# A diffusion block: the first modulation in two column parts, and one block turned by DMA

## The chip, the cores and the metric

The kernel runs on one core of a Trainium2 chip. The metric is device time in microseconds, the median of several executions. The engines are PE (TensorE matmuls), PEld (its weight loads), DVE (VectorE), ACT (ScalarE), POOL (GpSimd) and SP (SyncE, which here only issues transfers; ACT issues some too).

## The reference

One token block of a diffusion transformer with adaptive layer norm: 2048 tokens, width 640, 32 heads of 20, a sliding window of 256 keys, and a gated MLP of width 1536. Cut to what matters:

```python
mod = (silu(c) @ w_mod).reshape(1, 6, 1, 640)     # c: 1 x 640, w_mod: 640 x 3840
sa, ca, ga, sb, cb, gb = the six parts of mod
h = layernorm(x) * (1 + ca) + sa                   # first modulation: sa and ca
qkv = h @ wqkv                                     # 640 x 1920, q, k, v of 32 heads
p = softmax(mask(q k' / sqrt(20)))                 # causal, 256 keys back
x = x + ga * ((p v) @ wo)
h = layernorm(x) * (1 + cb) + sb                   # second modulation
x = x + gb * ((sigmoid(h @ w_gate) * (h @ w_up)) @ w_down)
```

## The kernel before, in words

The 2048 tokens are worked on in eight chunks of 256, each of two blocks of 128 (block 0 and block 1). For a chunk: layer norm of both blocks with tokens on partitions, a turn to `hT` (features on partitions, five tiles `dt` of 128), the modulation as a scale and a shift per partition, the projections to q, k and v (token blocks times weight halves of 320 columns), a turn of q and k to `QT` and `KT`, scores, exponential, masks, the product with V, normalization, output projection, second norm, and the MLP. Chunks overlap: the projections of the next two chunks and the MLP of earlier ones are interleaved on PE with the scores.

The order of the work is not found at run time and not by the loops. The loops only record operations with their reads and writes, each on an engine or a choice of engines. `PLAN` (L365) is a table of numbers that gives for every step which recorded operation comes next and on which engine; `schedule` walks the table and `emit` turns it into one program per engine, with semaphore waits worked out from the reads and writes. So each engine works strictly in its own order, and what waits blocks what stands behind it. SP's transfers stand in one queue in order of issue. The table has one entry for each of some 2000 operations.

What the change touches, by lines of the kernel before:

- `load_x` (L606) loads a block of x; the first two go out at once, one from SP and one from ACT. `load_bulk` (L621) loads weights in pieces by input tile. The first modulation's 1280 columns of `w_mod` (shift and scale, 640 each) come in five pieces of 128 x 1280 (L646) into the room of `wd`, which is free then.
- `load_w3` (L632) loads wq: tiles 0 to 2 of the left half first of all, then the right half, then tiles 3 and 4 of the left half.
- `silubc` (L662 to L669) is silu(c), turned by PE (`ctr`), halved by DVE into `c_col`, through a tanh on ACT and a product on DVE, and spread to 64 columns on ACT.
- `warm` (L676) is matmuls on zeros at the start, `fill` (L687) single ones on zeros between the first real steps.
- `modA` (L760 to L779): for each of five input tiles `kt`, ten 64-column matmuls of `w_mod` against `silubc` into one PSUM tile; then one DVE copy to `mA`, five shift columns and five scale columns.
- `pe_transposes` (L843) turns chunk 0 and 1's normalized x on PE through `ident`; `modulate` (L825) applies `mA` to chunk 0 in 128 x 128 pieces on DVE, ACT or POOL.
- `qkv` (L929) does the projections through `pe_chain` (L701), whose `step` says how many of the five input tiles stand in one PE operation, and turns q and k: on PE with an evacuation by ACT or DVE for chunks below `NPQ`, with a DMA transpose issued by SP for all others.
- Every plain matmul is recorded at L698, every one that uses a part of the array at L699, every plain DMA at L584, every DMA transpose at L822.

## Time and profile before

| what | value |
|---|---|
| median of 3 runs | 323.93 us (322.73 to 323.95) |
| profiled execution, first to last instruction | 321.83 us |
| median less that span | 2.1 us |
| PE busy | 315.6 us, 98% of the span, 5045 matmuls |
| DVE, ACT, POOL busy | 198.8, 213.9, 189.5 us |
| DMA | 32.92 MB, mean 102 GB/s |

The profiled execution's own time is its span, 321.83 us; the runs' times are device times that lie around such a span. PE is busy nearly throughout, so its busy share alone says little: what is to be looked for is where it is not busy, and which work is on it that could be elsewhere. The page's slices of 8 us show the DMA share at nine tenths or more up to about 88 us and then at a few tenths.

### The profile page before, as it was taken

What the parts mean: (1) busy time and instruction counts of PE and PEld (TensorE: products, weight loads), DVE (VectorE), ACT (ScalarE), POOL (GpSimd) and SP (SyncE); (2) the same over time, 40 slices, a digit from 0 to 9 for tenths busy, and PEclk for the clock granted to TensorE, in tenths of its full rate; (3) what the DMA queues carried; (4) which work ended last, traced back from release to release, by engine and by line L of the source; (5) the groups of instructions that cost most, each with busy time, mean ns of one, the idle gap of its engine ahead of it and who ended that gap; (6) DMA issues with size and microseconds to landing.
All of it is one profiled execution on the core that took longest, in us unless ns stands there. A gap on an engine that the chain in (4) does not pass through costs nothing.

```text
span 321.8 us, 11465 instructions
## 1 busy us (share of the span) xinstructions
PE 315.6 (98%) x5045; PEld 236.8 (74%) x5045; DVE 198.8 (62%) x424; ACT 213.9 (66%) x229; POOL 189.5 (59%) x349
## 2 busy tenths in 40 slices
PE   6999999999999999999999999999999999999996
PEld 2677767677877777766777677877877777877885
DVE  4689987877886746584555555465534474386323
ACT  2699997877787986768686867676976746411220
POOL 3338759878768493949484848577575826601000
PEclk9999999999999999999999999999999999999999
DMA  7999999999922534126526100220800004002101
GB/s 249 348 262 278 223 179 248 194 225 295 206 36 43 88 75 55 44 63 108 77 19 111 37 22 2 63 42 25 132 18 4 22 22 104 20 5 61 43 0 41
DMA packets 62123, 32.92 MB, mean 102 GB/s; under 512 B 45946, under 2 KB 60794, under 8 KB 62074
## 3 DMA queue, kind: packets, MB, share of 16 engines
q1 hardware_dynamic: 59904, 29.73, 43.5%
q10 hardware_dynamic: 2170, 2.46, 2.8%
q8 instruction: 39, 0.64, 0.9%
q14 instruction: 10, 0.08, 0.1%
HBM read 18.68 MB, written 2.62 MB: 66 GB/s over the span
## 4 chain that ended last, share of the span: by engine, by line
PE 96%; DMA 1%; DVE 1%; ACT 1%; issue 0%; ACTq 0%
PE M L698 79%; PE S L699 8%; PE M L699 7%; DMA x<-in_A_x_dram 1%; ACT hT L831 1%; DVE st L793 1%; PE S L698 1%; PE S L690 0%; ACT stg L914 0%; ACTq L584 0%; DVE x L815 0%; DVE st L795 0%; ACT hT L914 0%; DVE x L1308 0%; DVE mA L778 0%
## 5 line engine op out<-in xcount | busy, mean ns | idle before, releaser
L1067 ACT ACTIVATE E<-S 128x2048 bf16<-128x2048 f32 x56 | 105.0, 1875 | 40.6 <-PE S L699 40.2
L1072 POOL TENSOR_SCALAR_AFFINE_SELECT E<-E 128x256 bf16<-128x256 bf16 x112 | 46.6, 427 | 57.1 <-ACT E L1067 25.1
L1076 POOL TENSOR_SCALAR_AFFINE_SELECT E<-E 128x512 bf16<-128x512 bf16 x112 | 70.6, 646 | 4.6 <-DVE x L815 1.2
L698 PE MATMUL M<-h2T,wg 128*128 128x256 bf16 x480 | 67.0, 273 | 0.0
L698 PE MATMUL M<-h2T,wu 128*128 128x256 bf16 x480 | 66.7, 273 | 0.0
L1289 DVE SCALAR_TENSOR_TENSOR hh<-sig,M 128x512 bf16<-128x512 f32 x48 | 32.4, 678 | 42.9 <-ACT sig L1287 26.4
L698 PE MATMUL M<-wd,hh 128*128 128x320 bf16 (+2 forms) x396 | 57.1, 295 | 0.0
L698 PEld LDWEIGHTS M<-h2T,wg 128*128 128x128 bf16 x480 | 45.4, 98 | 7.8 <-DVE T L1162 0.2
L698 PEld LDWEIGHTS M<-h2T,wu 128*128 128x128 bf16 x480 | 45.2, 98 | 7.3
L1287 ACT ACTIVATE sig<-M 128x512 f32<-128x512 f32 x48 | 28.5, 595 | 31.2 <-PE M L698 30.9
L698 PEld LDWEIGHTS M<-wd,hh 128*128 128x128 bf16 x396 | 37.2, 98 | 13.7 <-DVE hh L1289 0.2
L1045 POOL TENSOR_SCALAR_AFFINE_SELECT E<-E 128x1024 bf16<-128x1024 bf16 x28 | 32.0, 1147 | 4.9 <-ACT E L1041 3.4
L699 PEld LDWEIGHTS S<-QT,KT 20*64 20x64 bf16 (+1 forms) x1856 | 20.0, 100 | 17.4 <-issue 9.7
L699 PE MATMUL S<-QT,KT 20*64 20x256 bf16 (+5 forms) x1856 | 32.3, 228 | 0.4 <-issue 0.4
L1041 ACT ACTIVATE E<-S 128x2048 bf16<-128x2048 f32 x14 | 26.3, 1876 | 6.8 <-PE S L699 6.7
L793 DVE BATCH_NORM_STATS2 st<-x 128x6 f32<-128x320 bf16 x64 | 28.9, 479 | 2.4 <-DMA x<-in_A_x_dram 1.8
L1162 DVE STREAM_TRANSPOSE T<-M 128x512 f32<-128x512 f32 x32 | 21.5, 700 | 12.9 <-PE S L699 11.6
L698 PE MATMUL M<-wk,hT 128*128 128x320 bf16 x160 | 27.9, 299 | 0.0
L1308 DVE TENSOR_TENSOR x<-M,x 128x320 bf16<-128x320 f32 (+2 forms) x33 | 15.4, 475 | 18.8 <-PE M L698 18.6
L698 PE MATMUL M<-wq,hT 128*128 128x320 bf16 x160 | 26.2, 299 | 0.7 <-DVE hT L832 0.5
L698 PE MATMUL M<-wv,hT 128*128 128x320 bf16 x160 | 26.0, 299 | 0.0
L698 PE MATMUL M<-wo,oT 128*128 128x320 bf16 x160 | 25.9, 299 | 0.0
(84 smaller groups left out, 356.4 us busy)
## 6 DMA issues: line engine op xcount, KB each, us to landing
x<-in_A_x_dram SPq DMA_DIRECT2D x18, 160.0 KB, 3.7
wd<-in_w_mod_dram SPq DMA_DIRECT2D x6, 320.0 KB, 5.4
wd<-in_B_w_down_dram SPq DMA_DIRECT2D x4, 480.0 KB, 5.5
wu<-in_w_mod_dram SPq DMA_DIRECT2D x5, 320.0 KB, 4.8
x<-in_A_x_dram ACTq DMA_DIRECT2D x8, 160.0 KB, 2.7
out_dram<-x SPq DMA_DIRECT2D x8, 160.0 KB, 1.9
wu<-in_B_w_up_dram SPq DMA_DIRECT2D x2, 576.0 KB, 4.7
wg<-in_B_w_gate_dram SPq DMA_DIRECT2D x2, 576.0 KB, 6.8
```

The source lines that it names most:

```text
L698: return e.matmul(o, l, r, start=st, stop=sp, skip_group_check=True)
L699: return e.matmul(o, l, r, start=st, stop=sp, tile_position=tp, skip_group_check=True)
L793: A("dve", lambda e, g, bi=bi, j=j: e.bn_stats(v(bi * 12 + j * 6, 6), src[bi].ap[:, j * 320:(j + 1) * 320]), 0.48, reads=[src[bi].r()], wr ...
L1041: A("act", lambda e, eng: e.activation(cell().rearrange("p m (x c) -> p m x c", c=64)[:, :, 0:4:3, :], Sp.ap[:].rearrange("p j (k x c) -> ...
L1045: A("pool", lambda e, eng, c0=c0, pat=pat, base=base, cm=cm: e.affine_select(cell()[:, :, c0:c0 + 64], cell()[:, :, c0:c0 + 64], pattern=p ...
L1067: A("act", lambda e, eng: e.activation(part(0, 512), Sp.ap[:], ACT.Exp, scale=SM_SCALE), 1.876, reads=[Sp.r()], writes=[E.r("C"), E.r("B") ...
L1072: A("pool", lambda e, eng, hc=hc, src=src, far_h=far_h: e.affine_select(side(hc), part(src, 64), pattern=[[0, 4], [-1 if far_h else 1, 64] ...
L1076: A("pool", lambda e, eng, c0=c0, near=near: e.affine_select(part(c0, 128), part(c0, 128), pattern=[[0, 4], [1 if near else -1, 128]], com ...
L1162: A("dve", lambda e, g, h=h: e.transpose(T1.ap[:, 512 * h:512 * h + 512], X[h].ap), 0.694, reads=[X[h].r()], writes=[T1.r(h)], prio=3.5, t ...
L1287: A("act", lambda e, g, pg=pg, sg=sg: e.activation(sg.ap[:], pg.ap[:], ACT.Tanh, scale=0.5), c_act(512), reads=[pg.r()], writes=[sg.r()], ...
L1289: A("dve", lambda e, g, pu=pu, sg=sg, f0=f0: e.scalar_tensor_tensor(out=hh.ap[:, f0:f0 + 2, :], in0=sg.ap[:].rearrange("p (a b) -> p a b", ...
L1308: A("dve", lambda e, g, ps=ps, bi=bi, c0=c0, n=n: e.tensor_tensor(x1[bi].ap[:, c0:c0 + n], ps.ap[:, 0:n], x1[bi].ap[:, c0:c0 + n], op=ALU. ...
```

## The change

- The first modulation is split by columns into tiles 0 to 2 (part 0, `CUT = 3`) and tiles 3 and 4 (part 1): in loading (six transfers in place of five, rows of 768 and 512 bytes in place of 2560), in multiplying (thirty matmuls, then twenty, each part with its own PSUM accumulation and its own copy to `mA`) and in applying (an operation on tile `dt` reads the copy of its part only).
- wq is loaded as tiles 0 to 2 in full width ahead of everything, and tiles 3 and 4 in full width later. Chunk 0's Q projection on PE is made in steps of three and two tiles.
- The warm-ups are seven groups with sixteen matmuls in place of eleven. The column `c_col` is gone: the tanh and the product read PSUM, with the half as a scale.
- PE turns q and k of chunk 0 and of chunk 1's block 1 (in the code's count, from 0); the other block of chunk 1, its first, is now turned by DMA.
- `PLAN` is another table for all engines. The planner's costs and latencies (`dlat`, durations of modulations and warm-ups) were changed too; they have no effect at run time besides the table.

Places where the order moves. First PE, from the turns of chunk 0's x to the first K projection; `S<-E` is warm-up and fill, `S<-silubc,wd` is `modA`, `M<-ident,x` turns x, `M<-ident,stg` turns q and k. Before:

```order
L690 MATMUL S<-E 128x512
L698 MATMUL M<-ident,x 128x128 x2
L690 MATMUL S<-E 128x512 x2
L698 MATMUL M<-ident,x 128x128 x3
L698 MATMUL S<-silubc,wd 128x64 x30
L690 MATMUL S<-E 128x512 x2
L698 MATMUL M<-wq,hT 128x320 x17
L698 MATMUL M<-ident,stg 128x128 x8
L698 MATMUL M<-wq,hT 128x320 x3
L698 MATMUL M<-wk,hT 128x320 x5
```

Now:

```order
L713 MATMUL M<-ident,x 128x128 x5
L713 MATMUL S<-silubc,wd 128x64 x12
L705 MATMUL S<-E 128x512 x2
L713 MATMUL M<-ident,x 128x128 x5
L705 MATMUL S<-E 128x512 x2
L713 MATMUL M<-wq,hT 128x320 x6
L713 MATMUL S<-silubc,wd 128x64 x20
L705 MATMUL S<-E 128x512
L713 MATMUL M<-wq,hT 128x320 x14
L713 MATMUL M<-wk,hT 128x320 x5
L713 MATMUL M<-ident,stg 128x128 x12
```

Six Q matmuls now stand ahead of part 1's twenty, all twenty Q matmuls stand ahead of any turn of q, and the eight turns that stood ahead of the first K projection now stand behind it.

Second, SP's queue at the start. Before:

```order
L584 DMA wq<-in_A_wqkv_dram 128x3x320
L584 DMA x<-in_A_x_dram 128x640
L584 DMA wd<-in_w_mod_dram 128x1280 x5
L584 DMA wq<-in_A_wqkv_dram 128x5x320
L584 DMA wq<-in_A_wqkv_dram 128x2x320
L584 DMA x<-in_A_x_dram 128x640 x2
L584 DMA wk<-in_A_wqkv_dram 128x5x320
```

Now:

```order
L590 DMA wq<-in_A_wqkv_dram 128x3x640
L590 DMA x<-in_A_x_dram 128x640
L590 DMA wd<-in_w_mod_dram 128x3x384 x2
L590 DMA wd<-in_w_mod_dram 128x2x384 x2
L590 DMA x<-in_A_x_dram 128x640
L590 DMA wd<-in_w_mod_dram 128x5x256 x2
L590 DMA x<-in_A_x_dram 128x640
L590 DMA wq<-in_A_wqkv_dram 128x2x640
L590 DMA wk<-in_A_wqkv_dram 128x5x320 x2
```

The first wq load is twice as large and ahead of x, part 0 follows x, and a block of x stands ahead of part 1 and another ahead of the rest of wq.

Third, SP further on, where the first DMA transposes stand. Before:

```order
L584 DMA wo<-in_A_wo_dram 16x3x640
L584 DMA wd<-in_w_mod_dram 128x3x640
L822 DMA_TRANSPOSE hT<-x 128x5x128 x2
L584 DMA wd<-in_w_mod_dram 128x2x640
L584 DMA gate<-grow 4x160
```

Now:

```order
L590 DMA wu<-in_w_mod_dram 128x1280 x2
L843 DMA_TRANSPOSE QT<-stg 128x8x128
L590 DMA wd<-in_w_mod_dram 128x3x640
L843 DMA_TRANSPOSE KT<-stg 128x8x128
L590 DMA hh<-in_w_mod_dram 128x3x640
L843 DMA_TRANSPOSE hT<-x 128x5x128 x2
L590 DMA wd<-in_w_mod_dram 128x2x640
L590 DMA gate<-grow 4x160
```

Two turns, of q and of k of chunk 1's first block, with loads between them, now stand ahead of the turn of chunk 2's `hT`.

The diff, cut to its core; of the table only one line:

```diff
 PLAN = [
-    119, 53, 76, 3, 8, 297, 86, 84, 300, 305, 333, 270, 277, 99, 281, 48, 442, 335, 28, 437, 447, 94, 13, 287, 422, 427,
...
-NPQ = 2
-PQ = ()
+NPQ = 1
+CUT = 3
+PQ = ((1, "q", 1), (1, "k", 1))
...
         if k == "wq":
-            for t0, t1 in ((0, 3), (3, 5)):
-                dma(lambda t0=t0, t1=t1: W3[k][:, t0:t1, 0:320], lambda t0=t0, t1=t1: wqkv_src[:, t0:t1, 0:320], 0.224 * (t1 - t0),
+            for t0, t1 in ((0, CUT), (CUT, NDT)):
+                dma(lambda t0=t0, t1=t1: W3[k][:, t0:t1, :], lambda t0=t0, t1=t1: wqkv_src[:, t0:t1, 0:D], 0.448 * (t1 - t0),
                     writes=R_wq0[t0:t1], prio=prio, tag=k)
...
-    load_bulk(wm_ap[0], wm_src[:, :, 0:1280], Rm[0], 0.88, 0.2, "wm0", dlat=2.89)
+    Rw = [[[R(f"wm0_{part}_{kt}_{b}") for kt in range(NDT)] for b in range(2)] for part in range(2)]
+    for part, (lo, hi) in enumerate(((0, 128 * CUT), (128 * CUT, D))):
+        k = 0
+        for m in (3, 5) if part == 0 else (5,):
+            for b in (1, 0):
+                dma(lambda k=k, m=m, lo=lo, hi=hi, b=b: wm_ap[0][:, k:m, b * D + lo:b * D + hi],
+                    lambda k=k, m=m, lo=lo, hi=hi, b=b: wm_src[:, k:m, b * D + lo:b * D + hi],
...
-    A("dve", lambda e, g: e.tensor_scalar(c_col[:], psc.ap[:, 0:NDT], 0.5, None, op0=ALU.mult), 0.17, reads=[psc.r()], writes=[R_ccol], prio=0)
-    A("act", lambda e, g: e.activation(cth[:], c_col[:], ACT.Tanh), 0.2, reads=[R_ccol], writes=[R_cth], prio=0)
+    A("act", lambda e, g: e.activation(cth[:], psc.ap[:, 0:NDT], ACT.Tanh, scale=0.5), 0.21, reads=[psc.r()], writes=[R_cth], prio=0)
...
-    for i in range(6):
-        o = A("pe", warm if i < 5 else lambda e, g: warm(e, g, 1), 1.03 if i < 5 else 0.52, prio=90, reads=[R_z], extra=wprev, tag="warm", writes=[R("w")])
+    for d, n in ((0.92, 2), (0.92, 2), (0.92, 2), (0.7, 2), (0.5, 2), (0.45, 2), (0.86, 4)):
+        o = A("pe", lambda e, g, n=n: warm(e, g, n), d, prio=90, reads=[R_z], extra=wprev, tag="warm", writes=[R("w")])
...
+    SPAN = ((0, CUT), (CUT, NDT))
...
+    for part, (lo, hi) in enumerate(SPAN):
+        n = (hi - lo) * MW
+        for kt in range(NDT):
+            def fnA(e, g, kt=kt, lo=lo, hi=hi, part=part, n=n):
+                for b in (1, 0):
+                    for cg in range(lo, hi):
+                        ins = mm(e, psA.ap[:, part, b * n + (cg - lo) * MW:b * n + (cg - lo + 1) * MW],
+                                 wm_ap[0][:, kt, b * D + cg * 128:b * D + cg * 128 + 128], silubc[:, kt, 0:MW], False, kt == NDT - 1)
+                return ins
+            if kt and part == 0:
+                fills.append(fill(FILL, oA[-1:]))
...
+        A("dve", lambda e, g, lo=lo, hi=hi, part=part, n=n: e.tensor_copy(
+            mA[:, :, lo:hi], psA.ap[:, part, 0:2 * n].rearrange("p (b a m) -> p b a m", b=2, m=MW)[:, :, :, 0]), 0.17,
+          reads=[psA.r(part)], writes=[R_mA[part]], prio=0)
...
-                A(MOE, mb, {"dve": 0.24, "act": 0.42, "pool": 0.38}, port=True, reads=Rmod, writes=[dst.r((dt, bi))], prio=prio,
+                A(MOE, mb, {"dve": 0.31, "act": 0.48, "pool": 0.45}, port=True, reads=[Rmod[dt >= CUT]] if len(Rmod) > 1 else Rmod, writes=[dst.r((dt, bi))], prio=prio,
...
-                             hold=[s, dst] + (pss if PAIR else []))
+                             hold=[s, dst] + (pss if PAIR else []), step=CUT if a == 0 and key == "q" else 2)
```

## The prediction

> **What bounds the kernel now.** I read the busy times of all engines by stage first, since the page's averages mix stages with different limits. Columns: the stretch in us, its length, busy us of PE, PEld, DVE, ACT, POOL with their instruction counts, granted clock, DMA share, GB/s.

> ```profile
> 1.31:6.00 4.69, 4.67 (x13) 1.46 (x13) 1.32 (x6) 1.49 (x2) 1.15 (x7) 1.00 0.84 263
> 6.00:7.47 1.47, 0.00 (x0) 0.00 (x0) 1.44 (x5) 0.47 (x1) 0.82 (x2) 1.00 1.03 368
> 7.47:11.22 3.75, 3.75 (x66) 2.56 (x66) 1.44 (x6) 1.07 (x3) 1.35 (x5) 1.00 1.08 375
> 11.22:11.71 0.49, 0.00 (x0) 0.03 (x1) 0.49 (x3) 0.49 (x2) 0.00 (x0) 1.00 1.14 367
> 11.71:13.95 2.24, 2.08 (x15) 1.31 (x16) 1.56 (x5) 2.09 (x6) 1.32 (x3) 1.00 1.15 320
> 15.19:60.00 44.81, 44.41 (x788) 31.33 (x786) 38.37 (x91) 40.06 (x49) 31.20 (x56) 1.00 1.09 237
> 60.00:319.40 259.40, 259.40 (x4153) 199.05 (x4151) 152.69 (x309) 167.59 (x167) 152.68 (x268) 1.00 0.34 68
> 319.40:321.83 2.43, 0.01 (x1) 0.00 (x0) 0.29 (x1) 0.00 (x0) 0.00 (x0) 1.00 0.26 81
> ```

> From 15.19 us, where the first K projection starts, to 319.4 TensorE is busy in all but 0.40 us, at the full granted clock. No other engine can be the bound there. So a time can come only from three places: when that dense stretch begins, how much PE work is in it, and new holes. The tail of 2.43 us ends with the same last add and store in both programs. In the dense stretch's first 45 us the DMA share is also at 1.09, so transfers are a second limit just behind PE.

> Second view, the waits, PE alone, from 13.9 us on: these two are all there are.

> ```profile
> PE S L699 <- issue: 0.4, 1, 0.4
> PE M L698 <- ACT stg L914: 0.2, 1, 0.2
> ```

> Third, what sets the beginning: issue times from the timeline, and time from issue to landing from the transfers of short windows.

> ```profile
> 1.82 2.34 SPq L584 DMA_DIRECT2D wd<-in_w_mod_dram  x5
> wd<-in_w_mod_dram SPq DMA_DIRECT2D x1, 320.0 KB, 5.1
> wd<-in_w_mod_dram SPq DMA_DIRECT2D x1, 320.0 KB, 6.5
> 7.54 0.45 SPq L584 DMA_DIRECT2D wk<-in_A_wqkv_dram  x1
> wk<-in_A_wqkv_dram SPq DMA_DIRECT2D x1, 400.0 KB, 6.7
> 10.83 0.17 DVE L778 COPY mA<-S 128x10 f32<-128x10 f32 x1 [1.46 <-PE S L698]
> 15.19 0.84 PE L698 MATMUL M<-wk,hT 128*128 128x320 bf16 x5
> ```

> The first of five modulation loads (the row of 5.1) is issued at 1.82 and lands at 6.9. The last (6.5) is issued near 3.7, because five issues share 2.34 us, and lands at 10.2. The modulation is copied out at 10.83, 0.6 later. The first K weights land at 7.54 + 6.7 = 14.2. Now bytes. Ahead of the first modulation landing lie 240 KB of wq, 320 KB of x and itself, 0.90 MB; ahead of the last 2.21 MB; ahead of the K weights 3.52 MB. So 1.31 MB of 2560-byte rows took 3.3 us (400 GB/s), and the next 1.31 MB, of 640- and 1280-byte rows, 4.0 us (327 GB/s). These two rates bound the changed loads, whose rows have 1280, 768 and 512 bytes.

> **The change part by part.** Loads first. The new order on SP is wq 480 KB, x, the modulation's columns 0 to 383 (576 KB, then 384 KB), block 2 of x, columns 384 to 639 (640 KB), block 3, the rest of wq (320 KB), K weights. Counting on from 0.90 MB landed at 6.9: part 0 is complete at 1.80 MB, which is 9.2 at 400 GB/s and 9.7 at 327; part 1 at 2.62 MB, 11.2 or 12.2; the rest of wq at 3.11 MB, 12.4 or 13.7; the K weights at 3.52 MB, 13.5 or 14.9. I take the slower rate, whose 640-byte rows are nearest in size, and shade it by 0.1. Part 0 is thus half a microsecond earlier than the whole was, and part 1 two later. [...]

> Then PE, from these rows (their starts give spacings):

> ```profile
> 7.80 0.47 PE L698 MATMUL S<-silubc,wd 128*128 128x64 bf16 x10
> 8.10 0.38 PE L690 MATMUL S<-E 128*128 128x512 bf16 x1
> 8.32 0.45 PE L698 MATMUL S<-silubc,wd 128*128 128x64 bf16 x10
> 14.34 0.61 PE L698 MATMUL M<-ident,stg 128*128 128x128 bf16 x8
> 14.79 0.57 PE L698 MATMUL M<-wq,hT 128*128 128x320 bf16 x3
> 15.87 0.33 PE L698 MATMUL M<-ident,stg 128*128 128x128 bf16 x3
> L831 ACT ACTIVATE hT<-hT,mA x4: 479/487/493, 11.0 to 12.7; 128x128 bf16<-128x128 bf16 x4
> L832 POOL TENSOR_SCALAR hT<-hT,mA x3: 452/452/453, 12.5 to 13.3; 128x128 bf16<-128x128 bf16 x3
> ```

> Ten modulation matmuls take 0.30, a fill 0.22, eight transposes 0.45 (0.056 each), five 320-column matmuls 15.19 to 15.87, 0.137 each. In the new order part 1's twenty matmuls (0.6) follow the first six Q matmuls. From part 1's landing at 12.1: twenty, 0.6; fill, 0.22; six Q matmuls of the second block, 0.82; eight of columns 3 and 4, 1.1. That gives 14.85, and with two semaphore steps, up to 15.1 for the first K matmul. The K weights, landing at 14.8, allow 14.9. Beside this lie the copy of part 1 (0.17) and the four remaining modulations, two each on ACT (0.49) and POOL (0.45), some 1.1 in all, against 1.04 of fill and Q matmuls: they fit, and cost about 0.1 if they do not. The c column that is no longer written, the product moved to DVE and the five more warm-ups end before part 0 lands; x lands 0.6 to 0.75 later behind the doubled wq, and its second block is normalized near 10, before the PE reaches its transposes. So they cost nothing, covered by the wait for part 0; without that cover the late x would cost its 0.7. **First term:** 15.19 becomes 15.1, -0.1 (14.6 to 15.9).

> **Second term.** Sixteen Q and K transposes of the first block of chunk 1 leave PE. But before, eight transposes of chunk 0 stood ahead of the first K matmul, and now none does. Inside the dense stretch 56 become 48: eight fewer, -0.45. The freed evacuations, about 0.6 each, lie on DVE and ACT beside PE and bring nothing by themselves. Changes between PE's four-row form and the full one are 154 in both orders, so the rest of the dense work is equal.

> **Third term,** new holes. The score tile has one buffer, and the next scores wait for the exponential of the last.

> ```profile
> 29.37 1.88 ACT L1104 ACTIVATE E<-S 128x2048 bf16<-128x2048 f32 x1 [0.43 <-PE S L699]
> 28.98 0.33 PE S L699 x8
> 31.33 0.37 PE S L699 x16
> 33.88 0.36 PE S L699 x24
> ```

> Scores start 2.35 and 2.55 apart here. Priced from the rows, the new order places two sets of chunk 0 and the first of chunk 1 about 2.25 apart; two times 0.1 is missing. I take +0.2 (0 to 1.5, the upper end if each of the first fifteen sets loses 0.1).

> Sum: -0.1 - 0.45 + 0.2 = -0.35. The profiled execution has a span of 321.83; the median run, 323.93, stands 2.1 above it, which I keep outside as unchanged. **Forecast 323.6 us.** A measurement of this kernel can tell about 0.5% (1.6 us) from no change, so this counts as the same.

> **Rivals.** First, the other side: the DMA turn is late. The scores of chunk 1 read K of its first block, and behind the waiting score matmul all of PE is queued.

> ```profile
> 29.32 1.47 PE M L699 x72
> hT<-x SPq DMA_TRANSPOSE x1, 6.5
> KT<-stg SPq DMA_TRANSPOSE x1, 4.3
> 33.81 0.43 PE L699 MATMUL S<-QT,KT 20*64 20x256 bf16 x24
> ```

> From the first K matmul to this first score of chunk 1 took 18.6; the new order has two projection matmuls more and eight transposes fewer, 18.45, so it is due at 33.55. Behind the last K matmul of that block stand 29 projection matmuls (4.0), eight transposes (0.45), three score sets (1.1) and the 72 matmuls of 1.47: it ends at 26.5, its evacuation about 0.7 later, and the turn, behind one more load on SP, is issued at 27.4. With 4.3 to 6.5 to landing it comes at 31.7 to 33.9: just hidden. Each us beyond 33.55 is paid in full. Slower than before from a landing at 34.0 on; at 8.5 us, two more than the longest here, 35.9 and **325.9**. For it: the DMA share of 1.09. Against: the rows.

> Second: transfers keep 400 GB/s. Part 1 at 11.2 lets PE pace the stage and K start at 14.6; if the 0.40 of instruction waiting also falls elsewhere, -0.6 - 0.45 - 0.4 + 0.1 gives **322.6**. [...]

> Third, the clock. Spacing of the warm-up matmuls' weight loads:

> ```profile
> 3.91 0.15 PEld L679 LDWEIGHTS S<-E 128*128 128x128 bf16 x1 [0.28 <-issue]
> 4.34 0.15 PEld L679 LDWEIGHTS S<-E 128*128 128x128 bf16 x1 [0.28 <-issue]
> ```

> They start 0.43 apart, half the speed of the 0.22 fill. If executions open at different times, eleven warm-ups may at times be too few, and the runs' spread (322.73 to 323.95) would be that; a longer warm-up, 1.31 to about 6.8 by eight matmuls of 0.43 and eight of 0.22, would give the fast run each time, 322.73 - 0.35 = **322.4**. For it: two of three runs lie together high. Against: this execution was at full speed before its work began. [...]

> Fourth: 512-byte rows go slower than any here, say 260 GB/s for part 1 (0.66 MB, 2.5 instead of 2.0) with the loads behind: K starts at 15.9, **324.4**.

> **How the numbers follow.** Forecast 0.50, late turn 0.14, quick transfers 0.13, clock 0.13, slow rows 0.10. Below 322.3 fall about a third to half of the two fast cases, 0.13 with the forecast's edge; above 325.5 three quarters of the late turn and the edges, 0.14; the rest, 0.73, is the same. The forecast's own range is 322.9 to 324.5. Reaching to the others until about 0.2 is left out gives 322.1 to 325.3.

> **What would show it.** Right: first K matmul at 14.9 to 15.3, 48 transposes left, no PE wait over 0.3 after it. Part 1's matmuls at 12 to 12.3 confirm the transfer rate; at 11.3 the second rival. A PE wait ahead of the first chunk 1 score shows the late turn. Wrong: a hole over 1 us in the dense stretch anywhere, or a K start outside 14.6 to 15.9.

## The result, and the profile after

| | before | changed |
|---|---|---|
| median of 6 runs, us | 323.22 (322.53 to 323.95) | 331.63 (329.06 to 333.49) |
| span of the profiled execution, us | 321.8 | 329.3 (its own time 331.06) |
| first K matmul, us | 15.19 | 14.50 |
| `ident,stg` transposes | 64 | 48 |

The ratio is 1.0243 (95% interval 1.0204 to 1.0281): slower, by 8.4 us, where 0.35 us faster was forecast. The spread of the runs has grown as well, from 1.4 to 4.4 us. Three runs further down (turn_only, fetch_shift, pile_moved) each had one execution in a slower state; their medians, like all the ratios, are those of the other executions.

Busy times of the changed kernel by stage (columns as in the prediction):

```profile
14.50:60.00 45.50, 44.09 (x776) 30.18 (x775) 38.23 (x89) 40.80 (x50) 30.08 (x52) 1.00 1.15 249
60.00:90.00 30.00, 27.17 (x406) 19.12 (x405) 17.45 (x36) 21.07 (x26) 20.70 (x38) 0.94 1.04 225
90.00:326.90 236.90, 235.17 (x3755) 180.66 (x3752) 130.65 (x262) 148.18 (x148) 134.29 (x237) 1.00 0.24 47
326.90:329.30 2.40, 0.06 (x2) 0.00 (x0) 0.29 (x1) 0.00 (x0) 0.00 (x0) 1.00 0.33 102
```

Before, PE stood idle for 0.40 us between its first K matmul and the tail. Now it is idle for 1.41, 2.83 and 1.73 us, and between 60 and 90 the mean granted clock is 0.94. The tail is unchanged (2.40 us; 2.43 before). The waits of PE from 14.5 us on, with the total, the number and the longest:

```profile
PE S L714 <- issue: 2.1, 1, 2.1
PE M L713 <- POOL h2T L861: 1.4, 1, 1.4
PE M L713 <- DMA wv<-in_A_wqkv_dram: 0.7, 1, 0.7
PE M L713 <- DMA QT<-stg: 0.6, 1, 0.6
PE M L714 <- issue: 0.5, 1, 0.5
PE M L714 <- POOL E L1097: 0.3, 1, 0.3
PE M L713 <- DMA KT<-stg: 0.2, 1, 0.2
PE M L713 <- DVE stg L936: 0.2, 1, 0.2
```

Eight holes stand where there was one (of the two waits listed for the kernel before, that of 0.2 lies ahead of its first K matmul), and they are spread from 19 to 213 us. The largest, in the timeline of PE:

```profile
11.73 0.75 PE L713 MATMUL S<-silubc,wd 128*128 128x64 bf16 x20
14.50 0.84 PE L713 MATMUL M<-wk,hT 128*128 128x320 bf16 x5
...
74.64 0.23 PE L714 MATMUL S<-QT,KT 20*128 20x64 bf16 x7
76.94 0.40 PE L714 MATMUL S<-QT,KT 20*128 20x64 bf16 x25 [2.06 <-issue]
```

It cuts one group of 32 score matmuls after the seventh. All 32 read the same two tiles, and the profile names no releaser, so late data is unlikely; the reading tested below is that the program itself is late. Instructions arrive as transfers too: 39 of them, of 16 KB each, come on queue q8, and by their number they are TensorE's, whose 10,070 matmuls and weight loads on record make one piece per 258. The queues between 59 and 74.5 us, and between 74.5 and 75 (packets, MB, share):

```profile
q1 hardware_dynamic: 7030, 3.03, 83.4%
q14 instruction: 1, 0.01, 0.2%
```

```profile
q1 hardware_dynamic: 85, 0.11, 99.5%
q8 instruction: 1, 0.02, 11.7%
```

No 16-KB piece came for 15 us; then one started at 74.6, and 2.3 us later TensorE went on. In the kernel before, one came at 67.5, when the trace has 1981 matmuls and weight loads of TensorE. Here it came after 2188. The hole has a second price: from 77.13 us on the granted clock is at half for 3.413 us. Busy times of this stretch and of one as long before and after it:

```profile
73.71:77.13 3.42, 1.36 (x41) 0.91 (x39) 3.13 (x6) 1.35 (x2) 1.67 (x4) 1.00 1.27 280
77.13:80.54 3.41, 3.41 (x37) 1.99 (x22) 1.62 (x4) 2.31 (x2) 1.52 (x3) 0.50 0.94 276
80.54:83.95 3.41, 3.41 (x51) 2.70 (x50) 1.13 (x3) 2.19 (x3) 1.40 (x2) 1.00 1.19 195
```

In the stretch after the hole the granted clock is 0.50, and 3.41 us do the work of 1.71: its eight 320-column matmuls at 78.20 take 2.34 us, the same eight in half_early, at a clock of 1.00, take 1.25. Four of the six runs have a mean clock of 0.995, which is one such stretch; their mean is 332.3 us, that of the other two 329.5. The difference, 2.8 us, is more than the 1.7 that such a stretch costs by itself.

The bill of the profiled execution: start -0.69, eight transposes fewer -0.45, holes after the K start 6.0 against 0.4 before, halved clock +1.7. That is +6.2; the span grew by 7.5. Most of the remaining 1.3 us lies in the same eight holes: the waits count from the modelled end of the matmul ahead of a hole. Measured from the start of one matmul to the start of the next, less the usual spacing of such a pair, the eight holes take 7.0 us and the one before 0.6, which leaves about 0.5 open.

### The profile page after: what moved, and what is told of

Read it like the earlier page. It is cut to its first block, busy times and chain, and to the rows that moved or that the text cites. A ratio compares the mean times of both kernels' runs of the same rounds, so it can differ in the third digit from the quotient of the medians.

```text
span 329.3 us, 11449 instructions
## 1 busy us (share of the span) xinstructions
PE 318.8 (97%) x5035; PEld 236.5 (72%) x5035; DVE 194.3 (59%) x412; ACT 215.0 (65%) x233; POOL 191.3 (58%) x353
## 3 DMA queue, kind: packets, MB, share of 16 engines
HBM read 18.68 MB, written 2.62 MB: 65 GB/s over the span
## 4 chain that ended last, share of the span: by engine, by line
PE 79%; DMA 8%; POOL 4%; DVE 3%; SPq 3%; issue 1%; ACT 1%; DVEq 0%; POOLq 0%
PE M L713 66%; PE S L714 7%; PE M L714 6%; SPq L590 3%; DMA wv<-in_A_wqkv_dram 3%; POOL E L1097 2%; DMA h2T<-x 2%; DMA gate<-grow 1%; DMA gbc<-gate 1%; DMA KT<-stg 1%; POOL E L1093 1%; DVE T L1183 1%; POOL E L1066 1%; ACT E L1088 1%; DVE x L836 0%
## 5 line engine op out<-in xcount | busy, mean ns | idle before, releaser
L713 PE MATMUL M<-h2T,wu 128*128 128x256 bf16 x480 | 70.2, 273 | 0.0
L713 PE MATMUL M<-h2T,wg 128*128 128x256 bf16 x480 | 68.6, 273 | 1.4 <-POOL h2T L861 1.4
L713 PE MATMUL M<-wd,hh 128*128 128x320 bf16 (+2 forms) x396 | 58.4, 295 | 0.0
L713 PEld LDWEIGHTS M<-wd,hh 128*128 128x128 bf16 x396 | 36.9, 98 | 13.7
L714 PEld LDWEIGHTS S<-QT,KT 20*64 20x64 bf16 (+1 forms) x1856 | 20.0, 100 | 19.1 <-issue 11.3
L1183 DVE STREAM_TRANSPOSE T<-M 128x512 f32<-128x512 f32 x32 | 21.6, 699 | 14.9 <-PE S L714 13.1
L713 PE MATMUL M<-wv,hT 128*128 128x320 bf16 x160 | 29.0, 310 | 0.9 <-DMA wv<-in_A_wqkv_dram 0.7
L713 PE MATMUL M<-wq,hT 128*128 128x320 bf16 x160 | 27.2, 299 | 0.2 <-DMA KT<-stg 0.2
L713 PE MATMUL M<-wo,oT 128*128 128x320 bf16 x160 | 26.7, 299 | 0.0
```

The source lines that it names most:

```text
L713: return e.matmul(o, l, r, start=st, stop=sp, skip_group_check=True)
L714: return e.matmul(o, l, r, start=st, stop=sp, tile_position=tp, skip_group_check=True)
L1183: A("dve", lambda e, g, h=h: e.transpose(T1.ap[:, 512 * h:512 * h + 512], X[h].ap), 0.694, reads=[X[h].r()], writes=[T1.r(h)], prio=3.5, t ...
```

## The experiments

All runs are shown as ratio to the kernel before, timed beside them on the same chip (its median was 323.1 to 323.8 us). In kernels made from the kernel before, line numbers are about five higher (L703 for L698); nothing but the part named is changed. Most edits are in the table of numbers that sets the order, so their diff is shown as the order of an engine.

**Which part costs?** The change taken apart: the start alone, the DMA turn alone, the later order alone, and both parts with the old order. The switch for the turn is this, and the table is that of the one kernel up to the first K projection and of the other behind it:

```diff
-NPQ = 2
-PQ = ()
+NPQ = 1
+PQ = ((1, "q", 1), (1, "k", 1))
```

> Only the changed start: the modulation in two parts, the wider Q weight load, more warm-ups, and the order up to the first K projection; Q and K of chunk 1's first block turned by TensorE and the later order of all engines as before. Theory O (the later order is what costs: SP's loads and turns come to stand so that TensorE meets them late): none of its holes is here, and the first K matmul comes at 14.5 as in the change instead of 15.2, so 322.3 to 323 us. Rival D (the start's finer rows and earlier TensorE work push a stretch that is already full of transfers over its edge): the loads behind are late with the old order too, holes of 0.5 us and more after 15 us, 325 us or above.

> Only the DMA turn: block 1 of chunk 1's Q and K turned by DMA, issued on SP where the second TensorE turn stood; start and later order as before. Theory O: eight to sixteen transposes leave TensorE (-0.45 to -0.9), the turns push what follows on SP by 2.5 us but nothing there is due so soon: 322.8 to 323.5 us, no wait over 0.3 ahead of the first scores of chunk 1. Rival D (two turns of 4 to 6 us more in a full stretch): a wait of 1 us or more on the turned K or Q or on the rest of the modulation behind it: 324.5 or above.

> Only the remade order after the first K projection, with the start and the TensorE turn of before. Theory O: the holes of the change stay, above all the one of 2 us near 75 us with the stretch of halved clock behind it and the late h2 of 1.5 us at 155: 328 us or above. Rival D: they go with the parts that are undone: 324.5 us or below, no hole over 1 us.

> Changed start and DMA turn together, with the later order of before. Theory O: the two gains add: 321.8 to 322.8 us. Rival D: the two burdens add on the transfers: 326 us or above, with waits on wv, on the rest of the modulation and on the turned K.

| kernel | median us | ratio (95%) |
|---|---|---|
| start_only | 324.12 | 1.0018 (0.9996 to 1.0040) |
| turn_only | 331.78 | 1.0251 (1.0216 to 1.0286) |
| order_only | 331.20 | 1.0226 (1.0190 to 1.0261) |
| parts_old_order | 332.99 | 1.0287 (1.0254 to 1.0319) |

The order alone costs as much as the whole change: theory O holds for it. The waits of order_only behind its start are of the same kinds, though the largest stands at another place (46.0 us, again inside one group of score matmuls, again with a halved stretch behind it, 0.50 from 48.56 to 51.97), and not near 75, where the expectation had it:

```profile
PE S L704 <- issue: 2.0, 1, 2.0
PE M L703 <- POOL h2T L845: 1.5, 1, 1.5
PE M L703 <- ACT QT L919: 1.1, 1, 1.1
```

But the gains that theory O promised for the parts are not there. The start is worth nothing by itself. In the change the K projection begins at 14.5; in start_only it begins at 15.39, because in the old order eight transposes stand first and wait for an evacuation. The wait in start_only:

```profile
PE M L713 <- DVE stg L936: 0.5, 1, 0.5
```

And the turn alone, which this test put on SP where the second TensorE turn had stood, costs about as much as the whole change, as it does together with the start (parts_old_order, with a wait of 6.3 on the same turn). Its wait in turn_only, and the issue of K in SP's timeline (start, length):

```profile
PE S L704 <- DMA KT<-stg: 6.4, 1, 6.4
```

```profile
35.99 1.25 SPq L827 DMA_TRANSPOSE KT<-stg  x1
```

**Is it the turn, or where it is issued?** In turn_early both turns go out as soon as Q and K are evacuated. In turn_undone the changed kernel turns them with TensorE again. The order of SP in turn_early against turn_only:

```diff
-L589 DMA wo<-in_A_wo_dram 16x2x640 x2
+L589 DMA wo<-in_A_wo_dram 16x2x640
+L827 DMA_TRANSPOSE KT<-stg 128x8x128
 L827 DMA_TRANSPOSE QT<-stg 128x8x128
+L589 DMA wo<-in_A_wo_dram 16x2x640
...
-L827 DMA_TRANSPOSE KT<-stg 128x8x128
```

> As turn_only, but the two DMA turns stand on SP as soon as Q and K are evacuated, ahead of the rest of the modulation and of the two x turns; nothing else differs from turn_only. Theory L (the 6.4 us wait of turn_only and its halved clock are only the late issue, 36.0 instead of some 27 us): K lands at 31 to 33 us, the wait falls to 0 to 1 us, 323 to 324.5 us. Rival D (any two turns more in this stretch cost): the loads behind come late instead, a wait of 1 us or more near 38 to 42 us, 325.5 us or above.

> The changed kernel, but Q and K of chunk 1's first block turned by TensorE as before (16 transposes and their four evacuations at the place of the DMA turns); start and later order as in the change. Theory O: the turn is worth -0.5 to +0.5 in this order, the holes stay: 330 to 332.5 us. Rival T (the two DMA turns are what delays the rest of the modulation and the fetch): the holes at 37.7 and 74.9 go, 327 us or below.

turn_early took 327.43 us (1.0131, 1.0114 to 1.0149): by its time as theory D had it, though the wait of 1 us or more that D put near 38 to 42 us is not there. The wait on the turn fell from 6.4 to 2.1 us but did not go. Its wait, and the two issues in SP's timeline:

```profile
PE S L704 <- DMA QT<-stg: 2.1, 1, 2.1
```

```profile
26.09 2.44 SPq L827 DMA_TRANSPOSE KT<-stg  x1
28.65 2.52 SPq L827 DMA_TRANSPOSE QT<-stg  x1
```

The second turn is issued at 28.65 and lands 6.0 us later, at 34.7; the scores were due at 32.8. The first turn holds SP for 2.44 us, but that costs the second only 0.5, since DVE's evacuation of Q ends at 28.16 in any case. The rest is that Q is ready late in this order and that its turn takes 6.0 to land, where it took 4.2 in turn_only. So at neither of the two places did the order of before have room for this turn. A wait of 1.0 on an ACT result near 76 us is new as well, and the loss of 4.4 us is more than both waits. In the change Q goes out at 24.79 and K at 28.77, land after 5.8 and 4.0 us, and no score waits. turn_undone took 331.01 (1.0223, 1.0168 to 1.0277), within the expectation of theory O. The holes at 37.7 and 74.9 are gone from its trace, as rival T had said, but others of 1.7 (a K turn), 1.6 (h2) and 1.1 us (an evacuation of Q) stand in their place: the loss of the change does not hang on the turn, while the place of a single hole shifts with any edit.

**Early or late?** The first exponential of chunk 3 has the same place in both orders, so they can be joined there. By the traces it starts at 101.2 us before and at 107.1 in the change; the expectations put it too early.

> The changed kernel up to the first exponential of chunk 3 (about 94 us before, 104 us in the change; the same place in both orders), and the order of the kernel before from there on. Theory O2 (the change loses 4 to 5 us ahead of this place, to late transfers and one late piece of instructions, and about 3 us behind it, where SP is quiet, to the order of POOL, ACT and DVE): 328 to 329 us, no hole over 0.4 us after 105 us. Rival (all of the loss comes from the crowded transfers of the first 90 us and the rest follows from it): 330.5 us or above.

> The kernel before up to the first exponential of chunk 3, and the remade order from there on. Theory O2: the holes of 1.4 us near 150 and of 0.6 us near 205 are there without any crowding ahead of them: 325.5 to 327 us. Rival: 323 to 324 us.

half_early took 327.44 us (1.0135, 1.0095 to 1.0174), half_late 327.33 (1.0128, 1.0108 to 1.0148). The two halves add up to the whole (4.4 + 4.3 against 8.4), so the late half is no consequence of the crowded start; theory O2 has the split right. The early half's loss is within its 4 to 5, though the time given for it (328 to 329) was too high; the late half's is above its 2.5 to 4. The late half's largest wait in half_late, at 150 us:

```profile
151.83 0.38 PE L703 MATMUL M<-h2T,wg 128*128 128x256 bf16 x2 [1.32 <-POOL h2T L845]
```

A wait of 0.6 us in half_late stands at the joint (102 us) and may be of the joint's making. half_early has a new wait of 0.8 us at 142, which theory O2 had excluded.

half_early also tells the clock apart from the hole. Its profiled execution has the hole too, at the very same matmul:

```profile
74.74 0.23 PE L714 MATMUL S<-QT,KT 20*128 20x64 bf16 x7
77.31 0.36 PE L714 MATMUL S<-QT,KT 20*128 20x64 bf16 x25 [2.34 <-issue]
```

and yet the clock stays at 1.00. Steps of 3.413 us (the length of the halved stretch in the change), counted from the first moment of half_early at full clock (4.13), cut the hole in two:

```profile
72.40:75.81 3.41, 2.57 (x47) 1.72 (x37) 2.76 (x6) 2.37 (x2) 2.44 (x5) 1.00 1.04 321
75.81:79.22 3.41, 1.91 (x38) 1.46 (x38) 3.00 (x5) 1.48 (x1) 0.92 (x2) 1.00 1.16 239
```

**Why is the piece of instructions late?** Three edits. fetch_shift cuts the warm-up matmuls, so that the pieces end at other places of the program:

```diff
-        for k in range(n):
-            ins = e.matmul(p_S.aps[0][:, 3, :], Eall[:, 0:128], Eall[:, 128:640], start=True, stop=True)
+        for k in range(4 * n):
+            ins = e.matmul(p_S.aps[0][:, 3, 0:128], Eall[:, 0:128], Eall[:, 128:256], start=True, stop=True)
```

pile_moved thins the loads issued ahead of it in the change, and pile_early puts two loads ahead of it in the kernel before. SP's order in pile_moved against the change:

```diff
 L590 DMA wu<-in_B_w_up_dram 128x2x768
-L590 DMA wd<-in_B_w_down_dram 128x3x640 x2
+L590 DMA wd<-in_B_w_down_dram 128x3x640
 L590 DMA gbc<-gate 128x640
-L590 DMA wg<-in_B_w_gate_dram 128x3x768
 L843 DMA_TRANSPOSE hT<-x 128x5x128
 L590 DMA x<-in_A_x_dram 128x640
-L590 DMA wd<-in_B_w_down_dram 128x3x640
+L590 DMA wg<-in_B_w_gate_dram 128x3x768
 L590 DMA wu<-in_B_w_up_dram 128x2x768
+L590 DMA wd<-in_B_w_down_dram 128x3x640 x2
```

> The changed kernel with each of the sixteen 512-column warm-up matmuls of the start cut into four of 128 columns: 48 matmuls and 48 weight loads more in the program, the same columns, nothing else. It moves the places in TensorE's program at which a 16-KB piece of instructions is due, by 96 rows. Theory F (the piece that is due at 70.2 us is served only at 74.6, behind 2.0 MB of loads issued since 68.4, so TensorE runs dry for 2.06 us and the clock is then halved for 3.41 us): the piece comes due near 65 us, ahead of the pile; hole and halved clock go, -3.8 in a run that had both: 327.3 to 328.5 us. Rival (the hole belongs to the instruction at 74.88, whatever the fetch): 331 to 332 us, the hole of 2 us stays at its instruction.

> The changed kernel with 0.96 MB of the loads of 68.4 to 71.2 us (one third of the gate weights, one of the down weights) issued behind the next x block, 5 us later, on SP; no other engine's order is changed. Theory F: 1.0 MB is left ahead of the fetch, it is served by 72.5, the hole at 74.9 is below 0.5 us and the clock stays at 1.0: 327.3 to 328.7 us. Rival (the hole does not hang on the loads): 331 to 332 us.

> The kernel before with two loads of 576 KB issued on SP ahead of the two h2 turns instead of behind them, 3 us earlier. Theory F: the piece of instructions that is due at 67.5 us, and was served at once, stands behind them and is served at 70 to 72; at 72 TensorE runs dry for 0.5 to 1.5 us and a halved clock may follow: 324 to 327 us. Rival (instructions are not held up by loads): served at 67.5 as before; then at most the h2 turns are late, a wait on h2 and not on instructions.

fetch_shift took 328.20 us (1.0144, 1.0119 to 1.0170): no work removed, 48 matmuls added, and by the ratios 3.2 us faster than the change. The hole at the eighth matmul is gone, the piece came at 66.8. So the hole belongs to the fetch and not to its instruction. pile_moved took 328.99 (1.0155, 1.0117 to 1.0194), just above its range, and its profile lacks the hole as well, but not for the reason given: the piece still came only at 73.6; TensorE was 1.4 us later by then, through other holes, and just did not run dry. pile_early took 324.97 (1.0048, 1.0032 to 1.0064), and speaks against the pile: with both loads ahead of it, the piece came at 68.6, when the trace has 1986 matmuls and weight loads (1981 before), and what PE waited for was h2, whose turn landed at 72.9, and not instructions (ACT's and PE's timeline; PE's releaser is only what POOL ended last):

```profile
72.94 1.58 ACT L844 ACTIVATE h2T<-h2T,shB,scB 128x256 bf16<-128x256 bf16 x3 [2.94 <-DMA h2T<-x]
...
74.78 0.38 PE L703 MATMUL M<-h2T,wg 128*128 128x256 bf16 x2 [0.68 <-POOL st L812]
```

Six kernels have the same TensorE program up to this place, and the size of the hole goes by where TensorE stood when the piece began to come (its matmuls and weight loads on record until then):

| kernel | piece starts, us | TensorE at record | wait at the eighth score matmul, us |
|---|---|---|---|
| mended | 72.3 | 1959 | none |
| h2_later | 71.3 | 2079 | none |
| pile_moved | 73.6 | 2132 | none |
| mended_two | 73.5 | 2168 | 1.15 |
| changed | 74.6 | 2188 | 2.06 |
| half_early | 74.9 | 2203 | 2.34 |

TensorE goes on 2.3 to 2.7 us after the piece started, in all three with a wait. That the late piece makes the hole is thereby shown. What makes it late is not: h2_later and the change issue the same loads in the same order ahead of it, and its piece came 3.3 us sooner.

**Can the order be mended, hole by hole?** mended makes five moves in the change; h2_later makes one, on TensorE; mended_two joins that one with two of the five. SP's moves for the first 40 us in mended, and PE's in h2_later:

```diff
 L843 DMA_TRANSPOSE QT<-stg 128x8x128
 L590 DMA wd<-in_w_mod_dram 128x3x640
+L590 DMA wd<-in_w_mod_dram 128x2x640
+L590 DMA hh<-in_w_mod_dram 128x3x640
 L843 DMA_TRANSPOSE KT<-stg 128x8x128
-L590 DMA hh<-in_w_mod_dram 128x3x640
 L843 DMA_TRANSPOSE hT<-x 128x5x128 x2
-L590 DMA wd<-in_w_mod_dram 128x2x640
```

```diff
-L713 MATMUL M<-wd,hh 128x320 x20
-L713 MATMUL M<-h2T,wg 128x256 x2
-L713 MATMUL M<-wd,hh 128x320 x4
+L713 MATMUL M<-wd,hh 128x320 x24
 L714 MATMUL S<-QT,KT 64x256 x8
...
-L713 MATMUL M<-h2T,wg 128x256 x8
 L713 MATMUL M<-wo,oT 128x320 x7
+L713 MATMUL M<-h2T,wg 128x256 x10
```

> The changed kernel with five moves in its order and no other difference: the loads of pile_moved; on POOL and ACT the last two h2 modulations ahead of a mask and of an exponential, for the hole of 1.4 us at 155; on SP the turn of h2 behind the Q and K turns at 63 us, for the holes at 67 and 68.7; wv ahead of an x block, for the hole at 19.2; the rest of the modulation ahead of the K turn at 28.8, for the hole at 37.7. Theory O (the order of SP, POOL and ACT against TensorE's is what costs): -3.8 - 1.1 - 0.9 - 0.6 - 0.5 = -6.9, so 324 to 325.5 us. Rival D (the transfers themselves are too many for the first 90 us): each hole that is closed opens another, 328 us or above.

> The changed kernel with the first ten gate matmuls of the third h2 (the ones that waited 1.4 us at 155) put behind the next scores and seven output matmuls on TensorE, about 2 us later; ACT's next exponential moves ahead of one sigmoid with it. Theory O2 (7 us from turn to first use is too short in this order, the kernel before has 10): the hole goes and nothing waits in its place, -1.0 to -1.5: 330.1 to 330.7 us. Rival (the chain through POOL, ACT and the score tile is full, as in mended): another wait of 0.7 us or more within 10 us of it, 331 to 332 us.

> The changed kernel with the moves of pile_moved and h2_later and the h2 turn behind the Q and K turns at 63 us, without the two early moves of mended that put loads ahead of the K turn. Theory O2: -3.8 - 1.3 - 0.9, so 325.5 to 326.5 us. Rival D: other late transfers take their place, 328 us or above.

mended took 330.93 us (1.0228, 1.0171 to 1.0285), h2_later 328.06 (1.0189, 1.0121 to 1.0257), mended_two 328.99 (1.0165, 1.0128 to 1.0202). mended and mended_two did not come near the sum of the holes they were to close, as rival D had said; h2_later came out below both of its forecasts. In mended, the two loads put ahead of the K turn delay it: it is issued at 29.34 instead of 28.77 and takes 7.2 us to land instead of 4.0. In its place on PE stands, at 34 us:

```profile
PE S L714 <- DMA KT<-stg: 2.3, 1, 2.3
```

and the mean clock of that execution is 0.995, one halved stretch. So a wait of 0.5 us at 37.9 was traded for one of 2.3. In h2_later the wait on h2 is gone as both theories said, and two others are there, as the rival said:

```profile
152.04 0.43 PE L714 MATMUL S<-QT,KT 20*64 20x256 bf16 x24 [0.59 <-ACT E L1088]
...
157.72 1.50 PE L714 MATMUL M<-E,V 128*32 128x256 bf16 x64 [0.90 <-POOL E L1097]
```

That it is nonetheless 3.6 us faster than the change by the medians, which neither theory had, is mostly the early part, where nothing was edited: in three of its four runs the mean clock is 1.0, and the fourth, with a halved stretch, took 332.18. The two intervals overlap, and among runs at clock 1.0 the gain is 1.6 us (327.9 against 329.5). How much of it the move itself brought is not shown.

**Has the kernel before any slack?** start_long lets the changed start reach up to the first scores, past the evacuation that stopped start_only; spare_load adds 320 KB:

```diff
+    spare = sb("spare", [128, 1280])
+    dma(lambda: spare[:], lambda: wm_src[:, 4, 1280:2560], 0.86, writes=[R("spare")], tag="spare")
```

> As start_only, but the changed start reaches up to the first scores of chunk 0 instead of the first K projection, so that the eight transposes that made TensorE wait 0.49 us for an evacuation ahead of the K projection stand behind it as in the change. Theory O2 with a start that is worth something: first K matmul at 14.5, and 0.5 to 0.7 us of it reach the end: 322.6 to 323.2 us. Rival D (TensorE earlier by 0.7 us runs into transfers that are no earlier): a new wait of 0.5 us or more on wv or on the rest of the modulation, 323.3 to 324.3 us.

> The kernel before with one more load of 320 KB, into a tile that nothing reads, issued on SP behind the second of the next modulation's five loads (near 19 us). Theory D (the stretch up to 90 us has no slack in its transfers: 320 KB at the 350 GB/s of the loads puts everything behind it 0.9 us back): new waits on landings between 20 and 50 us, 324.0 us or above. Rival S (slack there; only the order of the change is at fault): 322.8 to 323.6 us, no new wait over 0.3 us.

start_long took 325.09 us (1.0063, 1.0041 to 1.0086), slower than either theory has it. K starts at 14.34, 0.85 earlier than before, and at 28 us all of it is lost and more, to evacuations on DVE and not to transfers:

```profile
27.13 0.84 PE L714 MATMUL M<-wq,hT 128*128 128x320 bf16 x5
28.87 0.40 PE L714 MATMUL M<-ident,stg 128*128 128x128 bf16 x4 [0.90 <-DVE stg L937]
29.66 0.58 PE L714 MATMUL M<-wv,hT 128*128 128x320 bf16 x3 [0.39 <-DVE V L937]
```

spare_load took 324.21 us (1.0030, 1.0011 to 1.0049): about the 0.9 us that 320 KB take at 350 GB/s (the mean of the kernel before from 7.47 to 15 us), and above 324.0, but the only new wait is one of 0.41 at 68 us on a Q turn, none between 20 and 50. The stretch holds little slack, not none; the expectation of theory D had the size right and the place wrong.

## Why the prediction was wrong

**First term (-0.1).** Sign right, size off: K started at 14.50, -0.69, outside the range of 14.6 to 15.9. Part 1 landed at 11.4 (issued at 4.9, 6.5 to landing), where 12.1 was forecast. My count of bytes was wrong, and not on the side of the rate. I counted on from 0.90 MB at 6.9 us, the bytes that stood ahead of the first landing; the trace of before has 1.57 MB moved by then, and the changed one 1.52, so parts of later transfers had moved too. From 6.9 to the landing the changed kernel moved 1.44 MB, not 1.72, at a mean of 320 GB/s, below the 327 that I chose. The sum's two semaphore steps, up to 0.25 us, are shown by no run: from the landing of part 1 to its first matmul (11.73) passed some 0.3 us, and from there to the K start 2.77, where the sum's matmuls and fill make 2.74. From 8 to 11 us, when mostly 512-byte rows moved, it was slower still (306 in start_only, which has the same loads). The stretch in the changed kernel, then in the one before:

```profile
DMA packets 1546, 0.92 MB, mean 307 GB/s; under 512 B 59, under 2 KB 1546, under 8 KB 1546
DMA packets 1325, 1.11 MB, mean 371 GB/s; under 512 B 73, under 2 KB 1236, under 8 KB 1325
```

So the fourth rival was right that such rows go slower here than any that I had looked at (307 GB/s against 327 and 400), and wrong in the size (260) and in the late K start. The second rival's start (14.6) came true without its condition, the 400 GB/s, and its time (322.6) did not. But start_only and start_long show that a start 0.7 us earlier is worth nothing here: the next evacuation takes it back. My sum passed it to the end undiminished.

**Second term (-0.45).** 48 transposes are left, as counted. Their worth cannot be seen apart; turn_undone (331.0 against 331.6 for the change) puts the whole turn within what the runs tell apart.

**Third term (+0.2, 0 to 1.5): the step that failed.** In the profiled execution it should have been about +8.6: 6.4 us of holes more than before, counted from start to start, 1.7 of halved clock, and 0.5 that is open. The 331.63 lies above every rival too. I priced "order of all engines remade" by one row only, the spacing of score sets in the first 15 sets, and gave its upper end from the same row. Three things were left out. The late half of the program, which I did not cost at all, loses 4.3 us by itself. The order of SP among loads and turns in the early half decides which of them is late; I checked it for one turn and one load. And what a hole costs besides its length, the halved clock, was treated only for the warm-up. Behind all three stands one reading: the list of waits of before, 0.6 us in all, was taken as a sign that work is covered. It says only that, in that order, nothing was late. start_long, turn_early and spare_load show how little was to spare.

**First rival (late turn, 325.9 at 0.14).** Its mechanism is real and its place was right, in another order: with the order of before the turn makes PE wait 6.4 us, or 2.1 when issued at once. Its landing time of up to 6.5 us holds (6.3 and 6.0 in turn_early), and what is late is paid at least in full: the wait there is 2.1 us, the loss 4.4. In the change itself the remade order had made room for it, and the loss came from elsewhere.

**Third rival (clock).** The longer warm-up brought nothing: start_only has it too and took 324.12, against 323.63 beside it. What I had wrong is where the clock matters: not in the first 7 us but where PE was idle for 2.0 us or more within one step of 3.413 us (2.06 in the change).

**What would show it wrong** was named as a hole over 1 us in the dense stretch or a K start outside 14.6 to 15.9. Both happened.

**Left open.** What makes a piece of instructions late (loads ahead of it do not suffice, by pile_early and h2_later), and how the late half's loss divides among POOL, ACT and DVE. No version that beats the kernel before was found; start_only is its equal.

## What to carry to other kernels

A profile without waits does not show slack: before pricing a remade order, look for each engine how long the thing that came last had been there before it was used, and price the order as unknown over the whole program, on the slow side above all, where the old one was free of waits. In a kernel that is dense to 0.4 us, a gain at one place reaches the end only if everything behind it can move up by as much. Test a change of order by joining the two orders at a place where both are in the same state; here two such runs told more than three mends of single holes.

## What the runs showed of the hardware that was not expected

```profile
31.08:34.49 3.41, 1.66 (x12) 0.98 (x10) 1.69 (x4) 2.18 (x2) 3.38 (x3) 1.00 1.31 238
34.49:37.91 3.42, 0.00 (x0) 0.00 (x0) 0.00 (x0) 0.00 (x0) 0.51 (x1) 1.00 0.83 210
37.91:41.32 3.41, 2.16 (x33) 1.49 (x34) 0.69 (x1) 1.42 (x1) 0.00 (x0) 0.50 0.98 249
41.32:44.74 3.42, 3.42 (x15) 1.81 (x13) 2.49 (x6) 1.48 (x4) 0.82 (x2) 0.50 0.42 103
44.74:48.15 3.41, 3.15 (x135) 2.28 (x134) 1.59 (x4) 2.79 (x3) 1.83 (x5) 1.00 0.38 80
```

In the step ahead of the halved one TensorE was idle for 2.06 of 3.42 us in the change, and for all 3.42 in turn_only.

**TensorE's own program travels with the data.** In the changed kernel 39 pieces of 16 KB come over the DMA engines, one in about 260 matmuls and weight loads, and a piece that started late stopped TensorE in the middle of a group, with no releaser in the profile (2.06 us here, 1.15 in mended_two, 2.34 in half_early). The profile names this "issue"; not every such wait is one, since the one of 0.5 us that ends at 38.4 has its last piece 4.4 us earlier.
